# Score matmuls as TensorE loops with a register-held address, in the middle pairs of three layers

## The chip, the cores and the metric

The kernel runs on one core of one Trainium2 chip. The metric is the device time of one execution in microseconds (us); three runs of the kernel before took 1979.33, 1980.79 and 1981.32 us, so its median is 1980.79 us. A core has five engines that run their own instruction streams and meet through semaphores: TensorE (PE, with its weight loads shown apart as PEld), VectorE (DVE), ScalarE (ACT), GpSimd (POOL) and SyncE (SP), which here issues the transfers from the chip's memory (HBM) to 16 DMA engines.

## What is computed

Four layers of attention for one token, A and B in turn: layer 0 is A, 1 is B, 2 is A again and 3 is B again. Each has 32 heads of 192 values and a cache of 8192 keys and values per head.

```python
def _A_ref(x, k_cache, v_cache, wq, wo):
    B, Sq, D = x.shape                      # 1, 1, 640
    q = (x @ wq).reshape(B, Sq, Hq, Dh) ... # Hq 32, Dh 192
    scores = jnp.einsum("bhqd,bhkd->bhqk", q, k) * (Dh ** -0.5)
    p = _softmax(scores, axis=-1)
    o = jnp.einsum("bhqk,bhkd->bhqd", p, v)
    return (o, back to one row) @ wo

x = x + _A_ref(_layernorm(x), A_k_cache, A_v_cache, A_wq, A_wo)
x = x + _B_ref(_layernorm(x), B_k_cache, B_v_cache, B_wq, B_wo)
x = x + _A_ref(_layernorm(x), A_k_cache, A_v_cache, A_wq, A_wo)
x = x + _B_ref(_layernorm(x), B_k_cache, B_v_cache, B_wq, B_wo)
```

Nearly all of the data is the caches, in bf16: with the weights, one execution reads 848 MB.

## The kernel before

**Pairs.** The 32 heads are worked on two at a time: `NPAIR` is 16 pairs per layer. The two heads of a pair lie on partitions 0 to 63 and 64 to 127; each partition holds `J` = 128 keys of 192 values. A pair's keys (6144 KB) fill two of the eight slots of the SBUF tensor `pool` (`NSLOT`, `slot`), one for each half `u` of `JU` = 64 keys per partition, and its values fill two more. So two pairs' worth of caches fit on the chip at once.

**The order.** The list `steps` (L245 to L304) sets what the engines do: for a pair `p` the scores of both halves (`products(p, 0)` and `products(p, 1)`), then `softmax(p)`, `values(p)` and `gather(p)`, then the next pair. Each engine's instructions are collected in a `Queue` in that order, with the semaphore waits that precede each of them (`Queue.settle` writes a wait into the list unless an earlier one covers it; `emit` sends them out). The list `plan` is the same for the transfers, all of which go through SP's queue; a transfer waits until the last reader of its slots has finished (`freed`, `before`). The keys of a pair are released by the last score matmul of a half (`freed[nt]`, L692), the values by the last matmul of `values` (L798).

**`products(p, u)`** (L663) is the part that is changed. VectorE multiplies the half's keys by the query, in place, in `NC` pieces along the 192 values of a head: two pieces of 96 in the middle pairs (`2 <= p < 14`) of layers 0, 1 and 3, four pieces of 48 elsewhere (L671). A piece is one instruction (L675). Then TensorE adds the products up: each matmul with the identity `ident` as its weights takes `R` = 8 of the 192 columns of all 64 keys (512 elements) and adds them into the PSUM bank `S` of that half. That is 12 matmuls per piece and 24 per half, each written out as an instruction of its own; before each piece PE waits for VectorE's piece (L683). The first matmul of a pair carries a weight load (L690); the others use `matmul_held` (L70 to L75), which adds a matmul without loading the weights again, so in the profile nearly all of them have the line L72. Their first one clears the bank (`start`), their last one signals.

**After the scores**, VectorE's reduction (L733, of both halves) sums the last 8 partial sums of every key, further small steps of DVE, PE and ACT make the softmax, PE multiplies the probabilities with the values (L790 and L72, tile `OY`), and VectorE folds the result (L814 and L816). VectorE executes in order, so its multiplication for the next pair (L675) stands behind L816 of this one. `q_spread` (L580) puts the next pair's query into PSUM; on PE it stands right behind the last score matmul.

Of the kernel before, what the change touches and what calls it, by code (L numbers as in the profile page):

```python
# [11 lines left out]
class Queue:  # L12
# [26 lines left out]
            for i, v in [(k, val), *implied[k].items()]:  # L39
                self.waited[i] = max(self.waited.get(i, 0), v)  # L40

    def op(self, fn, *events, sem=None, inc=1, signal=True, bank=(), holds=None):

        self.holds = holds
        for d in bank:
            self.wait(*[ev for q, ev in d.items() if q is not self])
        self.wait(*events)
        self.settle()
        if not signal:
            self.items.append((fn, None, 0))  # L50
            return None
        sem = self.sem if sem is None else sem
        n = self.counts[id(sem)] = self.counts.get(id(sem), 0) + inc
        self.known[id(sem), n] = dict(self.waited)
        self.items.append((fn, sem, inc))
        for d in bank:
            d[self] = (sem, n)
        return sem, n
# [11 lines left out]
def matmul_held(t, out, lhsT, rhs, start, stop, size=128, column=0):  # L70

    return t.add_instruction(mybir.InstMatmult(  # L72
        name=t.bass.get_next_instruction_name(), engine=mybir.EngineType.PE,
        ins=[t.lower_ap(rhs), t.lower_ap(lhsT, for_matmul_weights=True)], outs=[t.lower_ap(out)],
        start_tensor_calc=start, stop_tensor_calc=stop, tile_size=(128, size), tile_position=(0, column), ldweights=False))  # L75


PAIRS_W = 5
NSLOT = 8
# [3 lines left out]
def build(nc, A_x, A_k, A_v, A_wq, A_wo, B_x, B_k, B_v, B_wq, B_wo, out):  # L83
    _, H, SK, DH = A_k.shape
# [8 lines left out]
    R = 512 // JU  # L93
# [5 lines left out]
    TS = JU * DH  # L99
# [12 lines left out]
    with ExitStack() as ctx:  # L112
        def sb(name, shape, dt):
            return ctx.enter_context(nc.sbuf_tensor(name, shape, dt))
# [4 lines left out]
        def sem(name):  # L119
            return ctx.enter_context(nc.semaphore(name))  # L120

        ident = sb("ident", [P, P], BF16)
        pool = sb("pool", [P, NSLOT * TS], BF16)
        slot = [pool[:, i * TS:(i + 1) * TS] for i in range(NSLOT)]
        wq0 = [sb(f"wq0{i}", [P, DC, PD], BF16) for i in range(2)]
        rows = sb("rows", [P, QR], BF16)
# [49 lines left out]
        Su = [(use["S0"],), (use["S1"],)]  # L176
# [6 lines left out]
        PE = Queue(sem("pPE"))  # L183
# [8 lines left out]
        e = PO.op(lambda g: g.memset(ident[:], 0.0))  # L192
# [6 lines left out]
        e = PO.op(lambda g: g.memset(mask, 0.0))  # L199
        for t in range(G):  # L200
            e = PO.op(lambda g, t=t: g.affine_select(
                out=mask, in_=mask, compare_op=ALU.not_equal, fill=1.0,
                base=-32 * t, pattern=[[-1, 2], [-2, VK]], channel_multiplier=1), e)
# [7 lines left out]
        e = DV.op(lambda v: v.tensor_reduce(half[:], mask, AX.X, ALU.add), ev_mask)  # L211
# [7 lines left out]
        def first_load(kind, l, p):  # L219

            n = (kind, pair(l, p))
            if l >= 2 and n in KEPT[l - 2]:
                return (l - 2, ORDER[l - 2]["pairs"].index(n[1]))
            return (l, p)

        def stays(kind, l, p):
            return l < 2 and (kind, pair(l, p)) in KEPT[l]
# [17 lines left out]
        for l in range(NL):  # L245
# [8 lines left out]
            for p in range(NPAIR):  # L254
# [21 lines left out]
                if p < NPAIR - 2:  # L276
                    if first_load("v", l, p) == (l, p):
                        plan += [("v", l, p, u) for u in range(2)]
                        if l == 2 and p == 1:
                            i = plan.index(("k", l, 1, 0))  # L280
# [4 lines left out]
                    if p + 1 in (PAIRS_W, 2 * PAIRS_W):  # L285
                        b = (p + 1) // PAIRS_W - 1
# [18 lines left out]
        at = {n: i for i, n in enumerate(steps)}  # L305
# [11 lines left out]
        place, before, holder = {}, {}, [None] * NSLOT  # L317
# [31 lines left out]
        for g, (c0, k) in enumerate(Q_PARTS):  # L349
            i = plan.index(("wq", 2, g))  # L350
# [6 lines left out]
        for i, n in list(enumerate(plan)):  # L357
            if n[0] == "v" and n[3] == 0:
                m = n[:3] + (1,)
# [87 lines left out]
        def need(n):  # L447

            while n not in landed:
                m = plan[issued[0]]  # L450
                issued[0] += 1
                landed[m] = transfer(m)
            return landed[n]
# [22 lines left out]
        def busy(n):  # L476

            PE.wait(ev_const, last["S"][0])
            for i in range(n):
                PE.op(lambda t, i=i: (  # L480
                    t.matmul(SP_[0][:, :], lhsT=ident[:], rhs=ident[:].unsqueeze(1).broadcast_to([P, 4, P]), start=True, stop=True)
                    if i == 0 else
                    matmul_held(t, SP_[0][:, :], ident[:], ident[:].unsqueeze(1).broadcast_to([P, 4, P]), True, True)),
                    signal=False, bank=Su[0])
# [14 lines left out]
        def layer(l, ev_z, ev_true):  # L499
# [7 lines left out]
            if l == 2:  # L507
                busy(2)
            e = DV.op(lambda v: v.scalar_tensor_tensor(out=nv[:], in0=mv[:, 0:1], scalar=mv[:, 0:1], in1=mv[:, 1:2],
                                                       op0=ALU.mult, op1=ALU.subtract))  # L510
            e = DV.op(lambda v: v.tensor_scalar(vs[:], nv[:], -float(DH), float(DH) * EPS, ALU.mult, ALU.add), e, last["rs"])
# [6 lines left out]
            if l < 2:  # L518
                e = need(("wq", l, 0))
# [4 lines left out]
            else:  # L524
                e = ev_first[l - 2]
                q_first = wq0[l - 2]
            PE.wait(e)
            for c in range(DC):
                e = PE.op(lambda t, c=c: t.matmul(
                    QM[:, 0:PD], lhsT=xb[:, c:c + 1].broadcast_to([P, P]), rhs=q_first[:, c, :],  # L530
                    start=(c == 0), stop=(c == DC - 1)), signal=(c == DC - 1), bank=QMu)
# [131 lines left out]
            def products(p, u):  # L663
                nk = ("k",) + first_load("k", l, p) + (u,)
                nt = ("t", l, p, u) if stays("k", l, p) else nk
                kin = slot[place[nk]].rearrange("p (j d) -> p j d", d=DH)
                k3 = slot[place[nt]].rearrange("p (j d) -> p j d", d=DH)
                qi = (l * NPAIR + p) % 2
                DV.wait(need(nk), need(nt), ev_q[p])
                chunks = []  # L670
                NC = 2 if l != 2 and 2 <= p < NPAIR - 2 else 4  # L671
                QD = DH // NC
                for c in range(NC):
                    d0 = c * QD
                    e = DV.op(lambda v, d0=d0: v.tensor_tensor(  # L675
                        k3[:, :, d0:d0 + QD], kin[:, :, d0:d0 + QD],
                        q_sb[qi][:, d0:d0 + QD].unsqueeze(1).broadcast_to([P, JU, QD]), ALU.mult))
                    chunks.append(e)
                last["q"][qi] = chunks[-1]
                S = SP_[u]  # L680
                PE.wait(last["S"][u], ev_const)
                for c in range(NC):
                    PE.wait(chunks[c])  # L683
                    for r in range(QD // R):
                        d0 = c * QD + r * R
                        fin = c == NC - 1 and r == QD // R - 1
                        held = PE.holds is ident
                        e = PE.op(lambda t, d0=d0, fin=fin, held=held: (
                            matmul_held(t, S[:, :], ident[:], k3[:, :, d0:d0 + R], d0 == 0, fin) if held else
                            t.matmul(S[:, :], lhsT=ident[:], rhs=k3[:, :, d0:d0 + R], start=d0 == 0, stop=fin)),  # L690
                            signal=fin, bank=Su[u], holds=ident)
                freed[nt] = ev_S[p, u] = e  # L692
# [149 lines left out]
            for n in [n for n in steps if n[1] == l]:  # L842
                if n[0] == "m":
                    products(*n[2:])
                elif n[0] == "s":
                    softmax(n[2])
# [19 lines left out]
                elif n[0] == "wo":  # L866
                    k = NW - NB[l] if n[2] == 2 else NW
                    if l == 3 and n[2] == 0:
                        to_row()
                    e = (project_row if l == 3 or n[2] < 2 or NB[l] == 0 else project)(  # L870
                        n, slot[place[n]][:, 0:k * D], oT[:, 0:k], last["oTw"])
# [26 lines left out]
            e = DV.op(lambda v: v.tensor_tensor(x_true[:], x_true[:], YB[:, 0:DC], ALU.add), ev_y, ev_true, bank=YBu)  # L898
# [5 lines left out]
        e = SP.op(lambda s: s.dma_start(out[0, 0].rearrange("(h n) -> h n", h=2), ev_z[0:33:32, :]), ev_true, sem=semOUT, inc=16)  # L904
# [12 lines left out]
def bass_interleave_layers__gqa_block_cached__mha_block_cached__decode_kernel(  # L917
    nc: bass.Bass,
    A_x: bass.AP,
    A_k_cache: bass.AP,  # L920
    A_v_cache: bass.AP,
    A_wq: bass.AP,
    A_wo: bass.AP,
    B_x: bass.AP,
    B_k_cache: bass.AP,
    B_v_cache: bass.AP,
    B_wq: bass.AP,
    B_wo: bass.AP,
    out: bass.AP,
):  # L930
    build(nc, A_x, A_k_cache, A_v_cache, A_wq, A_wo, B_x, B_k_cache, B_v_cache, B_wq, B_wo, out)
# [28 lines left out]
```

## Time and profile before

| what | value |
|---|---|
| median of the runs | 1980.79 us |
| profiled execution | 1979.56 us |
| its span, first to last instruction | 1977.8 us |
| DMA packets of the data queue (q1) | 848.38 MB, 99.7% of the 16 engines' time |
| PE busy | 64% |
| DVE busy | 61% |
| ACT busy | 9% |
| mean granted TensorE clock | 0.789 of full speed |
| one piece of the multiplication (L675, 128x6144) | 3.36 us alone, 13.16 us for a pair's four |
| one issue of keys of 6144 KB, to landing | 34.8 to 35.8 us |

In a row of the profile the line and the engine come first, then the operation with its output and input tiles, the number of instructions, the busy time and the mean of one, and then the engine's idle time ahead of them with what ended it. Busy shares are means over the whole span. Matmuls overlap in their pipeline, so their records (0.38 us for one with 512 columns) are longer than the distance from one to the next. "DVE x <- PE y" in a table of waits means that VectorE stood idle until an instruction of PE was done; the columns are us in total, times, and the longest. Rows marked with a q (PEldq, SPq) are instructions that the engine's sequencer deals with by itself, such as waits on semaphores.

### The profile page before, as it was taken

Reading aid. Unit: us, or ns where it says so; the run is one execution under the profiler, and the core shown is the slowest. Engines: PE = TensorE matmul, PEld = TensorE weight load, DVE = VectorE, ACT = ScalarE, POOL = GpSimd, SP = SyncE. Lnnn points to the kernel's source line nnn. Section 1 sums busy time; section 2 is a strip of 40 time slices with the busy share of each in tenths; the row PEclk is TensorE's granted clock in tenths of the full one; section 3 lists DMA queues with packets and bytes.
Section 4 is the critical chain, followed back from the end, with each engine's and each line's share of the span. In section 5 each row is a group of like instructions: output and inputs, shape, how many; then the busy total and the mean of one; then the engine's idle time right before and its main releaser. Section 6 shows DMA issues by size and latency. Waiting matters only on the chain.

```text
span 1977.8 us, 12008 instructions
## 1 busy us (share of the span) xinstructions
PE 1267.5 (64%) x7742; PEld 127.0 (6%) x2599; DVE 1198.7 (61%) x812; ACT 168.2 (9%) x529; POOL 4.6 (0%) x24
## 2 busy tenths in 40 slices
PE   3567466566476566665786666666666667657668
PEld 0000000000100000000020000000001001000001
DVE  3567467467167656656756565665764765665756
ACT  0000000000000100100010000000000100000000
POOL 0000000000000000000000000000000000000000
PEclk9778787778677787777887777877787878777779
DMA  9999999999999999999999999999999999999998
GB/s 414 431 442 430 430 430 431 435 437 423 433 435 436 431 429 429 432 437 432 428 410 436 427 431 431 433 430 430 432 429 428 435 429 434 439 429 431 432 432 374
DMA packets 27095, 849.12 MB, mean 429 GB/s; under 512 B 3106, under 2 KB 3236, under 8 KB 3876
## 3 DMA queue, kind: packets, MB, share of 16 engines
q1 hardware_dynamic: 26900, 848.38, 99.7%
q8 instruction: 40, 0.66, 0.1%
q14 instruction: 11, 0.09, 0.0%
q10 hardware_dynamic: 144, 0.00, 0.0%
HBM read 848.36 MB, written 0.00 MB: 429 GB/s over the span
## 4 chain that ended last, share of the span: by engine, by line
DMA 58%; PE 25%; DVE 15%; ACT 1%; issue 1%; SPq 0%
DMA pool<-in_B_k_cache_dram 24%; DMA pool<-in_A_v_cache_dram 17%; DMA pool<-in_A_k_cache_dram 15%; PE S L72 14%; DVE pool L675 11%; PE OY L72 5%; PE OY L790 3%; DMA pool<-in_B_v_cache_dram 3%; DVE s_sb L733 1%; ACT p_sb L748 1%; DVE OY L814 1%; PE OY L628 1%; DVE acc L816 1%; PE S L690 1%; DVE m_bf L735 0%
## 5 line engine op out<-in xcount | busy, mean ns | idle before, releaser
L675 DVE TENSOR_TENSOR pool<-pool,q_sb 128x3072 bf16<-128x3072 bf16 (+1 forms) x360 | 837.6, 2392 | 151.0 <-DMA pool<-in_B_k_cache_dram 84.8
L72 PE MATMUL S<-pool,ident 128*128 128x512 bf16 x3004 | 782.9, 422 | 18.1 <-DVE pool L675 16.7
L814 DVE TENSOR_TENSOR OY<-OY,small 128x1536 f32<-128x1536 f32 x60 | 106.0, 1766 | 255.0 <-PE OY L72 254.9
L72 PE MATMUL OY<-pool,p_sb 128*16 128x512 bf16 x1920 | 206.0, 517 | 0.0
L828 PE MATMUL TB<-acc,small 128*33 128x192 f32 x120 | 46.3, 484 | 210.3 <-DVE acc L816 210.3
L733 DVE TENSOR_REDUCE s_sb<-S 128x128 f32<-128x1024 f32 x63 | 77.1, 1224 | 160.0 <-PE S L72 160.0
L690 PE MATMUL S<-pool,ident 128*128 128x512 bf16 x64 | 37.4, 584 | 212.4 <-DVE pool L675 212.3
L790 PE MATMUL OY<-pool,p_sb 128*16 128x512 bf16 (+1 forms) x1216 | 142.6, 490 | 45.3 <-DMA pool<-in_A_v_cache_dram 43.8
L542 ACT ACTIVATE q_sb<-QM 64x192 bf16<-64x192 f32 x120 | 38.9, 324 | 942.4 <-PE QM L580 941.7
L816 DVE TENSOR_REDUCE acc<-OY 128x192 f32<-128x1536 f32 x60 | 105.4, 1757 | 2.0
L837 ACT ACTIVATE rows<-TB,small 1x192 bf16<-1x192 f32 x120 | 49.5, 412 | 557.0 <-PE TB L828 555.5
L748 ACT ACTIVATE p_sb<-s_sb,small 64x128 bf16<-64x128 f32 x128 | 55.7, 435 | 172.1 <-DVE small L742 171.3
L804 DVE RECIPROCAL small<-TB 33x2 f32<-33x2 f32 x64 | 11.1, 173 | 94.3 <-PE TB L763 78.1
L738 PE MATMUL QM<-ident,m_bf 128*64 128x64 bf16 x128 | 14.0, 216 | 82.6 <-DVE m_bf L735 82.6
L763 PE MATMUL TB<-small,ones 128*33 128x2 f32 x120 | 14.4, 190 | 74.1 <-ACT p_sb L748 74.1
L580 PEld LDWEIGHTS QM<-rows,one_b 1*128 1x128 bf16 x60 | 5.5, 91 | 737.0 <-issue 731.0
L790 PEld LDWEIGHTS OY<-pool,p_sb 128*16 128x16 bf16 (+1 forms) x1216 | 34.6, 105 | 195.2 <-issue 138.5
L628 PE MATMUL OY<-pool,oT 128*1 128x320 bf16 x330 | 38.6, 411 | 2.2 <-ACT oT L658 2.2
L742 DVE TENSOR_REDUCE small<-QM 128x1 f32<-128x64 f32 x64 | 14.3, 224 | 27.8 <-PE QM L738 27.8
L828 PEld LDWEIGHTS TB<-acc,small 128*33 128x33 f32 x120 | 10.3, 133 | 297.9 <-DVE acc L816 292.0
L748 ACT ACTIVATION_READ_ACCUMULATOR p_sb<-s_sb,small 64x1 f32 x128 | 23.3, 182 | 0.0
L690 PEld LDWEIGHTS S<-pool,ident 128*128 128x128 bf16 x64 | 6.6, 103 | 249.8 <-DVE pool L675 246.8
(87 smaller groups left out, 245.2 us busy)
## 6 DMA issues: line engine op xcount, KB each, us to landing
pool<-in_B_k_cache_dram SPq DMA_DIRECT2D x28, 6144.0 KB, 35.8
pool<-in_B_v_cache_dram SPq DMA_DIRECT2D x28, 6144.0 KB, 31.0
pool<-in_A_v_cache_dram SPq DMA_DIRECT2D x27, 6144.0 KB, 26.9
pool<-in_A_k_cache_dram SPq DMA_DIRECT2D x34, 3072.0 KB, 20.4
pool<-in_A_k_cache_dram SPq DMA_DIRECT2D x14, 6144.0 KB, 34.8
pool<-in_A_v_cache_dram SPq DMA_DIRECT2D x9, 3072.0 KB, 13.8
pool<-in_B_k_cache_dram SPq DMA_DIRECT2D x8, 3072.0 KB, 22.4
pool<-in_A_wo_dram SPq DMA_DIRECT2D x6, 2400.0 KB, 20.9
```

The lines of the kernel that those rows point to most:

```text
L72: return t.add_instruction(mybir.InstMatmult(name=t.bass.get_next_instruction_name(), engine=mybir.EngineType.PE, ins=[t.lower_ap(rhs), t. ...
L542: lambda a, h=h, r=r, f=f: a.activation(q_sb[i][r, :], QM[r, h * DH:(h + 1) * DH], ACT.Copy, scale=f),
L628: e = PE.op(lambda t, i=i, h=h, f=l < 3 and n[2] == 0 and i == 0, fin=n == last_row and i == k - 1: t.matmul(YR[32 * h:32 * h + 1, :], lhs ...
L675: e = DV.op(lambda v, d0=d0: v.tensor_tensor(k3[:, :, d0:d0 + QD], kin[:, :, d0:d0 + QD], q_sb[qi][:, d0:d0 + QD].unsqueeze(1).broadcast_t ...
L690: t.matmul(S[:, :], lhsT=ident[:], rhs=k3[:, :, d0:d0 + R], start=d0 == 0, stop=fin)),
L733: lambda v: v.tensor_reduce(s[:], S_[:].rearrange("p (j r) -> p j r", r=R), AX.X, ALU.add),
L748: ev_p[p] = AC.op(lambda a, h=h, r=r: a.activation(p_sb[par][r, :, h], s[r, :], ACT.Exp, bias=negm[par][r, 0:1], accum_out=l_col[par][r, h ...
L790: t.matmul(o, lhsT=x, rhs=y, start=f, stop=fin) if c == 0 else
L814: e = DV.op(lambda v: v.tensor_tensor(o3, o3, pick[:, 0:VK].unsqueeze(2).broadcast_to([P, VK, DH]), ALU.mult), bank=Ou)
L816: e = DV.op(lambda v: v.tensor_reduce(acc[:], O.rearrange("p (i d) -> p d i", d=DH), AX.X, ALU.add), e, bank=Ou)
L828: e = PE.op(lambda t: t.matmul(TB[64:97, C_O:C_O + DH], lhsT=half33, rhs=acc[:], start=True, stop=True), bank=TBu)
L837: last["TO"] = last["row_written"] = AC.op(lambda a, h=h: a.activation(orow[:, o0 + h * DH:o0 + (h + 1) * DH], TB[64 + 32 * h:65 + 32 * h, ...
```

## The change

In the pairs with two pieces (12 pairs in each of layers 0, 1 and 3, so 36 pairs, 72 halves and 144 pieces) the matmuls of a piece are no longer all written out. Of a half's 24 matmuls the first and the last stay as they were. The other 11 of each piece are one matmul instruction in a loop on TensorE: its input address is held in the register `k_at0`, which a register addition moves on by 8 columns, and a compare-and-branch goes back until eleven rounds are done. The register is set ahead of the first piece's loop and runs on through the second. The wait for the second piece of the multiplication stands in the loop's body (`inside=True`), so it is executed in each of the eleven rounds; the wait for the first piece belongs to the single matmul ahead of the first loop. `Queue.op` takes the waits out of the list for that purpose and hands them to the function.

```diff
+        at = len(self.items)
         self.settle()
+        if inside:
+            waits, f = self.items[at:], fn
+            del self.items[at:]
+            fn = lambda eng: f(eng, waits)
...
+def matmul_loop(t, waits, out, lhsT, rows, first, count, regs, at, label, begin):
+
+    b, width, m = t.bass, out.shape[-1] // rows.shape[1], len(regs)
+    for i in range(m if begin else 0):
+        t.reg_mov(regs[i], at + 2 * (first + i * width))
+    with b.body(label, valid_engines=[mybir.EngineType.PE]):
+        for w in waits:
+            t.wait_ge(*w)
+        for reg in regs:
+            with b.discard():
+                v = bass.RuntimeValue.of_register_unchecked(reg, min_val=0, max_val=rows.shape[-1] - width)
+                x = t.lower_ap(rows[:, :, bass.ds(v, width)])
+            t.add_instruction(mybir.InstMatmult(
+                name=b.get_next_instruction_name(), engine=mybir.EngineType.PE,
+                ins=[x.__replace__(regref=reg.name, reg_ap_offset=reg.name), t.lower_ap(lhsT, for_matmul_weights=True)],
+                outs=[t.lower_ap(out)], start_tensor_calc=False, stop_tensor_calc=False, tile_size=(128, 128),
+                tile_position=(0, 0), ldweights=False))
+        for reg in regs:
+            t.reg_add(reg, reg, 2 * m * width)
+        t.br_lt(regs[0], at + 2 * (first + count * width), on_true=label, on_false=label + "_end")
+    b.switch_bb(label + "_end")
...
+        pool_at = nc.sbuf_base - 2 * NSLOT * TS
+        k_at = [nc.tensor.alloc_register(f"k_at{i}") for i in range(1)]
...
+                    if NC == 2:
+                        at = pool_at + 2 * TS * place[nt]
+                        n = QD // R
+                        m = len(k_at)
+
+                        def ends(d0):
...
+                        if c == 0:
+                            ends(0)
+                        PE.op(lambda t, waits, c=c: matmul_loop(
+                            t, waits, S[:, :], ident[:], k3, (m + c * (n - m)) * R, n - m, k_at, at, f"k_{l}_{p}_{u}_{c}", c == 0),
+                            signal=False, bank=Su[u], holds=ident, inside=True)
+                        if c == 1:
+                            e = ends(DH - m * R)
+                        continue
```

`ends` writes out the single matmuls (`m` is 1 here, the number of registers) in the form of before, and the last one signals. The arithmetic and its order are unchanged.

## The prediction

> **What bounds the kernel now.** First the page's shares and queues:
>
> ```profile
> PE 1267.5 (64%) x7742; PEld 127.0 (6%) x2599; DVE 1198.7 (61%) x812; ACT 168.2 (9%) x529; POOL 4.6 (0%) x24
> q1 hardware_dynamic: 26900, 848.38, 99.7%
> q8 instruction: 40, 0.66, 0.1%
> DMA 58%; PE 25%; DVE 15%; ACT 1%; issue 1%; SPq 0%
> ```
>
> No engine is full, the data queue is. So the kernel is bound by transfers, and removing work on TensorE can win only what it wins on the DMA engines. But a quarter of the chain of waits is PE: a pair is one serial chain of DVE and PE, and only if this chain is shorter than a pair's transfers does DMA stay the bound. The timeline of two pairs in layer 0 shows the chain:
>
> ```profile
> 95.45 13.16 DVE L675 TENSOR_TENSOR pool<-pool,q_sb 128x6144 bf16<-128x6144 bf16 x4 [2.73 <-DMA pool<-in_A_k_cache_dram]
> ...
> 99.27 12.15 PE L72 MATMUL S<-pool,ident 128*128 128x512 bf16 x47
> ...
> 111.45 1.23 DVE L733 TENSOR_REDUCE s_sb<-S 128x128 f32<-128x1024 f32 x1 [2.84 <-PE S L72]
> ...
> 119.38 1.76 DVE L816 TENSOR_REDUCE acc<-OY 128x192 f32<-128x1536 f32 x1
> ...
> 124.54 13.16 DVE L675 TENSOR_TENSOR pool<-pool,q_sb 128x6144 bf16<-128x6144 bf16 x4 [3.40 <-DMA pool<-in_A_k_cache_dram]
> ```
>
> The reader is to see that pairs start 29.1 us apart, that the next multiplication stands right behind L816, and that VectorE then waits 3.40 us for keys. These few microseconds per pair are all the room a longer chain has. The waits, by stretch (the middle pairs of layers 0, 1 and 3), give the whole of it:
>
> ```profile
> DVE s_sb L733 <- PE S L72: 38.7, 12, 5.1
> DVE pool L675 <- DMA pool<-in_A_k_cache_dram: 33.2, 13, 6.0
> ...
> DVE s_sb L733 <- PE S L72: 43.1, 13, 5.8
> DVE pool L675 <- DMA pool<-in_B_k_cache_dram: 38.1, 14, 8.3
> ...
> DVE s_sb L733 <- PE S L72: 41.0, 14, 3.8
> DVE pool L675 <- DMA pool<-in_B_k_cache_dram: 33.3, 12, 9.5
> ```
>
> VectorE waits (38.7+43.1+41.0)/39 = 3.15 us for the scores after its last piece: they end 13.16+3.15 = 16.3 us after the pair's start. And it waits 33.2+38.1+33.3 = 104.6 us for keys in all.
>
> Last, the pace of the score matmuls, in stretches of one pair (busy time and count of PE, then PEld and DVE; the first figure behind the brackets is the granted clock):
>
> ```profile
> 128.00:131.20 3.20, 3.20 (x8) 0.06 (x1) 0.00 (x0) 0.50 0.92 399
> 131.20:134.50 3.30, 3.30 (x11) 0.00 (x0) 0.00 (x0) 0.66 1.10 477
> 134.50:137.80 3.30, 3.30 (x17) 0.00 (x0) 0.00 (x0) 1.00 1.07 462
> ```
>
> After the idle time TensorE starts at half clock, then runs at full. At full clock 47 matmuls took 10.16 us in the tightest piece of the chain (at 693.46), 0.216 us each, so 0.43 at half. From the clocks 0.50, 0.66 here and 0.50, 0.86 in the pair at 873, some 10 to 13 of 48 matmuls are cold; I take 12. Check: 3.41 (first piece 3.36 and 0.05 to the first matmul) + 12 x 0.43 + 36 x 0.216 + 0.2 (the last one's drain) = 16.5 us, against 16.3 measured. So PE begins behind VectorE (a piece takes 13.16/4 = 3.29 us, 12 matmuls 0.27 us each), and uses its full speed to catch up.
>
> **The change, part by part.**
>
> Instructions removed: per half 24 matmuls become 2 single ones, 2 loop bodies and some set-up, about 12 fewer or a little less; 72 halves save about 900. The queue that feeds PE's instructions brought 0.66 MB for its 10341 records, 64 bytes each, so 0.06 MB less, 0.13 us at 429 GB/s. Bounds: nothing to the whole 0.1% share (2 us); I take 0.
>
> Address register, branch, wait: the loop runs 144 x 11 = 1584 rounds. In a round PE's sequencer deals with the matmul, a register addition, a compare-and-branch and, in the second piece of each half, the wait again. It can run ahead of the array, so a round costs the larger of the array's time and the sequencer's time q. The trace of before has no loop on PE, so q is bounded. Below: the array, 0.216 us. Above: three instructions as slow as the slowest that a sequencer handles here, the DMA issue on SP, 0.33 us: 1.0 us. The nearest rows are these (ns):
>
> ```profile
> L945 PEldq EVENT_SEMAPHORE  x1: 51/51/51, 0.7 to 0.7; - x1
> L945 SPq EVENT_SEMAPHORE  x1: 17/17/17, 0.7 to 0.7; - x1
> L112 SPq COMPARE_BRANCH  x1: 33/33/33, 1977.4 to 1977.4; - x1
> ```
>
> PE's sequencer takes 51 ns where SP's takes 17. A branch of 33 on SP, three times that on PE, is 0.10; addition and matmul at 0.05 each make 0.20, with the wait 0.25. Between consecutive issues SP's sequencer leaves about 0.06 (0.74 + 0.39 = 1.13 to 1.19 at the start of the run); three or four such gaps make q 0.38 to 0.49. I take the middle between 0.20 and 0.49, **0.33 us**, rather than the far bound of 1.0, because the small rows are of the same kind as the loop's instructions and the DMA issue is not.
>
> The Trainium skill (Advanced Engine Details and Errata, Control Flow Timing) puts a compare-and-branch at about 108 ns, near my 0.10; taken with 51 ns each for addition and matmul and no gaps, q would be 0.21 and the loop would cost nothing, which is the first rival's sum.
>
> Loop entry and exit: a register move and the branch that falls through, once each per loop, not shown either; between 0 and 0.33 us, I take 0.2 (four loops per pair, 0.8).
>
> Sum for a pair: 3.41 + 12 x 0.43 + 36 x 0.33 + 0.8 + 0.2 = 21.45 us, so the scores end 21.45 - 16.3 = 5.15 us later. PE no longer catches up with VectorE: in full-clock rounds it needs 0.33 where VectorE's pace is 0.27.
>
> What is late next: L733, the softmax, the values, L814, L816, and behind it on VectorE the next L675; on PE `q_spread` (L580) stands behind the last score matmul but has some 9 us in hand. On SP's queue the values' transfer (released by the scores) and the next keys' transfer (released by the values) are both issued 5.15 us later. A transfer of 6144 KB takes 14.7 us alone and 27 to 36 from issue to landing, so 12 us or more of queued work covers one such delay; it doesn't cover one in every pair.
>
> What hides it: VectorE's waits for keys. To the 104.6 us come 16.3 at the change from layer 0 to 1 and 3.7 in the last pairs, 124.6. Not all can be used (some lie ahead of the first changed pair); I take 115 us, 3.2 per pair. If this cover is gone, every microsecond counts in full. Layer 2 isn't changed.
>
> Total: 36 x 5.15 - 115 = 185 - 115 = +70 us on the profiled 1979.56, so 2050; the median shown is 1.2 above it, so **2051 us**. The sum is steep: 36 x 36 = 1300 us per us of q, or 13 us for every 10 ns. It is nil at q = 0.276, +18 at 0.29, +161 at 0.40.
>
> **The rivals.**
>
> *Hidden* (not slower). The round is within 0.27 us, so PE stays within the waits' cover: at q = 0.25 the scores end 2.3 us later, 83 us in all, less than 115. Time 1979 to 1981. For it: the small rows without gaps sum to 0.20 to 0.25, and DMA at 99.7% hides anything below 3.2 us per pair. Against it: gaps between instructions, and the cold start that uses up the catching-up already. It decides at q = 0.276.
>
> *Half clock.* The array idles within each round, and the granted clock stays at 0.50 through the scores, as it is in their first 3.2 us: a round is 0.43 whatever the sequencer does. 3.41 + 48 x 0.43 + 1.0 = 25.05, 8.75 later, 315 - 115 = +200: 2181 us. For it: at 144.58 the values' matmuls after a paced end ran at 1.07 us for eight where others took 0.60. Against it: in the cold state the array has no gaps at all when q is below 0.43, and the clock rose to 1.00 here although PE waited between pieces.
> The Trainium skill (TensorE: Matmul & The Clock Gate, Part 1) says the clock is raised after a busy window of about 3.4 us and lowered after an idle one; the 3.2 us at 0.50 agree, and by that rule gaps of a third of a round need not lower it, which is why this rival gets less than the forecast.
>
> *Heavy branch.* Going back makes the sequencer start its fetching anew, at about another 0.33 us: q = 0.6, 3.41 + 48 x 0.6 + 1.0 = 33.2, 16.9 later, 608 - 115 = +493, 2474 us. Nothing in the profile of before speaks for it but that no taken branch on PE is shown.
>
> *Faster.* Fewer instruction fetches leave the DMA engines more even; at most the 0.1% of q8 and q14, 2 us: 1979.
>
> **How the numbers follow.** Forecast (q from 0.28 to 0.40, 1985 to 2141 us) 0.49; hidden 0.26; half clock 0.17; heavy branch 0.05; faster 0.03. The likeliest gives 2051. The range goes from 1978, which takes in the hidden case, to 2181, the half clock; left out are the heavy branch, a part beyond the half clock and the small gains. Changes within 0.2% (4 us) can't be told from none in this kernel. Slower: 0.49 + 0.17 + 0.05 = 0.71; within 0.2%: 0.25; faster: 0.04, since a gain of over 4 us would need more than all instruction traffic.
>
> **What the changed profile would show.** The matmuls of the new line follow each other by about 0.33 us at full clock; L733's wait for PE rises from 3.15 to some 8.3 us in the changed pairs; VectorE's waits for keys there fall to nearly nothing; the pairs start 31 us apart instead of 29.1; q1's share falls to about 96%; the chain shows more PE and less DMA; layer 2 (965 to 1515 us) keeps its length. Wrong would be: rounds of 0.22 to 0.27 us with the keys' waits still there (hidden), a clock of 0.5 throughout the scores (half clock), or q8 with more packets than 40 (refetching).

## The result and the profile after

The changed kernel takes 2027.7 us (median of four runs, 2027.04 to 2033.93) against 1980.16 for the kernel before: a ratio of 1.0249, 95% interval 1.0236 to 1.0262 (ratios below are given in the same way, with the interval in brackets). The profiled execution has a span of 2025.2 us, 47.4 more than before. On its page, the queues and the chain of waits:

```profile
q1 hardware_dynamic: 26900, 848.38, 97.8%
q8 instruction: 36, 0.59, 0.1%
PE 50%; DMA 24%; DVE 22%; ACT 3%; issue 1%; SPq 0%
```

The same bytes took a smaller share of a longer span: DMA no longer binds all the time. PE's share of the chain has doubled. The four packets of instructions saved are there (36 instead of 40); the experiments below show whether they are worth anything.

One pair of layer 0, from its timeline (start, duration, engine, line; L95 is the loop's matmul, L77 a single one, L705, L785 and L868 are L675, L733 and L816 of before):

```profile
95.31 13.16 DVE L705 TENSOR_TENSOR pool<-pool,q_sb 128x6144 bf16<-128x6144 bf16 x4 [1.81 <-DMA pool<-in_A_k_cache_dram]
...
99.13 7.73 PE L95 MATMUL S<-pool,ident 128*128 x22
106.71 0.59 PE L77 MATMUL S<-pool,ident 128*128 128x512 bf16 x2
107.14 7.66 PE L95 MATMUL S<-pool,ident 128*128 x22
...
115.06 1.22 DVE L785 TENSOR_REDUCE s_sb<-S 128x128 f32<-128x1024 f32 x1 [6.58 <-PE S L77]
...
127.24 3.35 DVE L705 TENSOR_TENSOR pool<-pool,q_sb 128x6144 bf16<-128x6144 bf16 x1
```

VectorE waits 6.58 us for the scores where it waited 2.84, and the next pair's multiplication, at 127.24, has no wait for keys in brackets: the 3.40 us of before are gone, and the pair lasts 31.9 us instead of 29.1. The waits of all 36 changed pairs, by layer (0, 1 and 3; total, times, longest), say the same:

```profile
DVE s_sb L785 <- PE S L77: 81.3, 12, 7.9
DVE pool L705 <- DMA pool<-in_A_k_cache_dram: 1.8, 1, 1.8
...
DVE s_sb L785 <- PE S L77: 87.3, 12, 11.6
DVE pool L705 <- DMA pool<-in_B_k_cache_dram: 2.2, 2, 1.8
...
DVE s_sb L785 <- PE S L77: 81.4, 12, 8.4
```

VectorE waits (81.3 + 87.3 + 81.4) / 36 = 6.9 us per pair for the scores, and 4.0 us in all for keys, where it was 104.6. The sequencer's own rows, and PE's busy time and count with the granted clock behind them, in four stretches of this pair:

```profile
L101 PEldq ALU_OP  x1584: 36/36/42, 98.8 to 1960.0; - x198
L102 PEldq COMPARE_BRANCH  x1584: 76/208/340, 98.9 to 1960.1; - x198
```

```profile
98.60:104.20 5.60, 5.47 (x14) 0.54 1.00 430
104.20:106.60 2.40, 2.37 (x10) 1.00 1.33 573
106.60:110.60 4.00, 3.98 (x14) 1.00 0.91 393
110.60:114.60 4.00, 3.95 (x12) 1.00 0.97 418
```

The branch is the long one: 208 ns in the median, and 76 in the last round of each of the 144 loops, where it isn't taken. In the trace a round at full clock is 0.363 us: the addition 0.036, a gap of 0.060, the branch 0.207, and 0.06 until the next addition, in which the matmul is sent on. That is longer than the array's 0.216, so PE waits for its own sequencer. The stretches show where that holds (their counts include matmuls that only reach into a stretch). At half clock (the first) a matmul takes the array 0.43 us, so the array is the slower one and the sequencer runs ahead. When the clock rises, at 103.8 us, the matmuls sent ahead start 0.216 us apart until none is left, at 105.1, and from there on it is the sequencer's pace, 0.36 apart within a loop. The sequencer shows no pause while the array is cold: this pair's 44 additions start from 98.82 to 114.43 us, 43 rounds of 0.363 in the mean, and over all 36 pairs this mean has the median 0.362.

By pair, over the 36 changed ones (sums of the trace's start and end times):

| | before | after | difference, us |
|---|---|---|---|
| start of a pair to L733 / L785, mean | 16.49 | 20.10 | 36 x 3.60 = +129.7 |
| from there to the end of L816 / L868, mean | 11.01 | 11.36 | +12.9 |
| from there to the start of the next pair, sum | 86.5 | -1.4 (records overlap) | -87.9 |
| the rest: mostly waits at the change from layer 0 to 1 | | | -7.2 |
| span | 1977.8 | 2025.2 | +47.4 |

In the second row it is the matmuls with the values that grew. In this pair, before (the first line) and after, eight of them took:

```profile
115.00 0.60 PE L72 MATMUL OY<-pool,p_sb 128*16 128x512 bf16 x8
118.82 1.07 PE L77 MATMUL OY<-pool,p_sb 128*16 128x512 bf16 x8
```

The granted clock was 1.00 there before, and 0.50 after.

### The profile page after: what moved, and what is told of

Read it like the earlier page. It is cut to its first block, busy times and chain, and to the rows that moved or that the text cites. A ratio compares the mean times of both kernels' runs of the same rounds, so it can differ in the third digit from the quotient of the medians.

```text
span 2025.2 us, 15248 instructions
## 1 busy us (share of the span) xinstructions
PE 1407.0 (69%) x7742; PEld 129.9 (6%) x2599; DVE 1195.4 (59%) x812; ACT 168.1 (8%) x529; POOL 4.6 (0%) x24
## 3 DMA queue, kind: packets, MB, share of 16 engines
q1 hardware_dynamic: 26900, 848.38, 97.8%
## 4 chain that ended last, share of the span: by engine, by line
PE 50%; DMA 24%; DVE 22%; ACT 3%; issue 1%; SPq 0%
PE S L95 25%; DMA pool<-in_A_v_cache_dram 14%; DVE pool L705 11%; PE OY L77 7%; PE S L77 6%; DMA pool<-in_A_k_cache_dram 5%; DMA pool<-in_B_k_cache_dram 5%; PE OY L842 5%; DVE OY L866 4%; DVE acc L868 4%; DVE s_sb L785 3%; ACT p_sb L800 2%; PE OY L658 2%; PE S L725 1%; DVE m_bf L787 1%
## 5 line engine op out<-in xcount | busy, mean ns | idle before, releaser
L705 DVE TENSOR_TENSOR pool<-pool,q_sb 128x3072 bf16<-128x3072 bf16 (+1 forms) x360 | 836.9, 2391 | 63.9 <-DMA pool<-in_A_k_cache_dram 36.0
L95 PE MATMUL S<-pool,ident 128*128 x1584 | 536.7, 430 | 4.5 <-issue 2.2
L77 PE MATMUL S<-pool,ident 128*128 128x512 bf16 x1420 | 382.2, 421 | 10.5 <-DVE pool L705 9.8
L785 DVE TENSOR_REDUCE s_sb<-S 128x128 f32<-128x1024 f32 x63 | 77.1, 1224 | 291.8 <-PE S L77 291.8
L77 PE MATMUL OY<-pool,p_sb 128*16 128x512 bf16 x1920 | 214.8, 537 | 0.0
L842 PE MATMUL OY<-pool,p_sb 128*16 128x512 bf16 (+1 forms) x1216 | 151.1, 520 | 43.4 <-DMA pool<-in_A_v_cache_dram 43.4
L868 DVE TENSOR_REDUCE acc<-OY 128x192 f32<-128x1536 f32 x60 | 105.4, 1757 | 2.0
L725 PE MATMUL S<-pool,ident 128*128 128x512 bf16 x36 | 21.3, 593 | 78.3 <-DVE pool L705 78.3
L790 PE MATMUL QM<-ident,m_bf 128*64 128x64 bf16 x128 | 14.1, 218 | 82.6 <-DVE m_bf L787 82.6
L742 PE MATMUL S<-pool,ident 128*128 128x512 bf16 x28 | 16.0, 570 | 53.6 <-DVE pool L705 53.6
## 6 DMA issues: line engine op xcount, KB each, us to landing
pool<-in_A_k_cache_dram SPq DMA_DIRECT2D x14, 6144.0 KB, 29.9
```

The source lines that it names most:

```text
L77: return t.add_instruction(mybir.InstMatmult(name=t.bass.get_next_instruction_name(), engine=mybir.EngineType.PE, ins=[t.lower_ap(rhs), t. ...
L95: t.add_instruction(mybir.InstMatmult(name=b.get_next_instruction_name(), engine=mybir.EngineType.PE, ins=[x.__replace__(regref=reg.name, ...
L705: e = DV.op(lambda v, d0=d0: v.tensor_tensor(k3[:, :, d0:d0 + QD], kin[:, :, d0:d0 + QD], q_sb[qi][:, d0:d0 + QD].unsqueeze(1).broadcast_t ...
L725: t.matmul(S[:, :], lhsT=ident[:], rhs=x, start=f, stop=fin)), signal=fin, bank=Su[u], holds=ident)
L785: lambda v: v.tensor_reduce(s[:], S_[:].rearrange("p (j r) -> p j r", r=R), AX.X, ALU.add),
L842: t.matmul(o, lhsT=x, rhs=y, start=f, stop=fin) if c == 0 else
```

## The experiments

The theory: the sequencer's round, above all its branch, sets the pace of the score matmuls, and what the scores' lateness costs is its sum over the pairs less VectorE's waits for keys. The rivals: the register-held address makes the matmul itself slow; and every round costs its share of the 47.4 us wherever it stands. Times stand against runs of the kernel before on the same chip: 1979.42 us for the first four, 1979.71 for the others.

**What in the round costs: the branch removed.** The eleven matmuls and additions are written out, with the same register. The wait of a second piece then stands once ahead of its matmuls instead of in every round.

```diff
-    with b.body(label, valid_engines=[mybir.EngineType.PE]):
-        for w in waits:
-            t.wait_ge(*w)
+    for w in waits:
+        t.wait_ge(*w)
+    for k in range(count // m):
         for reg in regs:
...
-        t.br_lt(regs[0], at + 2 * (first + count * width), on_true=label, on_false=label + "_end")
-    b.switch_bb(label + "_end")
```

> The same register-held matmuls and register additions written out, no branch. If the branch sets the round, the sequencer needs 0.363 - 0.208 - 0.05 = about 0.10 us per matmul with its addition, the array's 0.216 binds, and the time is that of the kernel before, 1978 to 1983 us. If the register-held address or the addition is what costs, it stays near 2028 us.

It took 1981.04 us, ratio 1.0008 (0.9998 to 1.0017): no difference shown, and at most 0.17%. The second half of the same pair (L783 is the L785 of the changed kernel):

```profile
107.47 4.91 PE L95 MATMUL S<-pool,ident 128*128 x22
112.22 0.38 PE L77 MATMUL S<-pool,ident 128*128 128x512 bf16 x1
112.63 1.23 DVE L783 TENSOR_REDUCE s_sb<-S 128x128 f32<-128x1024 f32 x1 [3.74 <-PE S L77]
```

The 22 register-held matmuls took 4.91 us, 0.216 apart, where the loop's took 7.66. The register-held address and the addition are free here; the branch is not.

**Two matmuls per round.** `for i in range(2)` in the line of `k_at`: five rounds of two matmuls per piece.

> Two registers, so two matmuls per round and five rounds per piece. If the branch sets the round (a round of 0.363 us, of which the branch and the gaps around it are all but one matmul's dispatch of 0.06 and one addition's 0.10), a round of two takes 0.363 + 0.06 + 0.10 = 0.52 us, 0.26 per matmul, below VectorE's 0.274: scores end at most 1 us later than in the kernel before, the time is 1980 to 1984 us. If the matmul with a register-held address is itself slow, two of them take 0.7 us, and the time stays near 2028. If each executed round costs a fixed 0.030 us (47.4 us over 1584 rounds), 720 rounds cost 22 us: 2002.

It took 1980.1 us, ratio 1.0003 (0.9993 to 1.0012). Its sequencer and the same pair's timeline:

```profile
L101 PEldq FUSED_REGOPS  x720: 37/37/42, 99.2 to 1909.8; - x180
L102 PEldq COMPARE_BRANCH  x720: 69/201/333, 99.3 to 1909.9; - x180
```

```profile
99.87 6.87 PE L95 MATMUL S<-pool,ident 128*128 x20
106.58 1.03 PE L77 MATMUL S<-pool,ident 128*128 128x512 bf16 x4
107.44 4.48 PE L95 MATMUL S<-pool,ident 128*128 x20
```

The branch takes as long as ever, but the two additions became one instruction, and consecutive branches start 0.37 us apart: the second matmul, with its addition, costs the sequencer 0.01 us, not the 0.06 + 0.10 expected. At 0.19 per matmul the array binds: the last 20 looped matmuls run at 0.216 each, and the scores are at L785 16.8 us after this pair's start (95.62).

**Three matmuls per round.** `range(3)`: three rounds per piece.

> Three registers: three matmuls per round, three rounds per piece. The branch is shared by three, the array binds, and the time is that of the kernel before and of two registers: 1978 to 1982 us. If fewer instructions to fetch were worth something, this or the kernel of two registers would be below the kernel before by more than 1 us; I expect that neither is.

It took 1979.7 us, ratio 0.9998 (0.9989 to 1.0008). Neither loop that keeps up is faster than the kernel before.

**A second addition per round, next to the first.** The addition is split into two in a row.

```diff
-            t.reg_add(reg, reg, 2 * m * width)
+            t.reg_add(reg, reg, m * width)
+            t.reg_add(reg, reg, m * width)
```

> The loop of the changed kernel with its addition done in two halves: one more sequencer instruction per round. If the sequencer's round is the bound and VectorE's waits are already used up, the round grows by about 0.10 us (an addition of 0.036 and its gap of 0.06), 44 rounds per pair by 4.3 us, 36 pairs by 154: 2182 us. If rounds are bound by the array, or by something that runs beside the additions, nothing changes: 2028.

It took 2027.43 us, ratio 1.0245 (1.0228 to 1.0262), as the changed kernel. This is no evidence for the second case of the expectation: the trace has 1584 additions, one per round, so the two had been combined and the question stayed open.

**A second addition, apart from the first.** Half a step is added ahead of the matmul and half behind it, and the register starts half a step lower.

```diff
-        t.reg_mov(regs[i], at + 2 * (first + i * width))
+        t.reg_mov(regs[i], at + 2 * (first + i * width) - width)
...
+            t.reg_add(reg, reg, m * width)
             with b.discard():
...
-            t.reg_add(reg, reg, 2 * m * width)
-        t.br_lt(regs[0], at + 2 * (first + count * width), on_true=label, on_false=label + "_end")
+            t.reg_add(reg, reg, m * width)
+        t.br_lt(regs[0], at + 2 * (first + count * width) - width, on_true=label, on_false=label + "_end")
```

> One addition of half a step ahead of the matmul and one behind it, so that two additions stand in every round and can't be combined (in the trace of the run with the addition split in two, each round still had one). If the sequencer's round is the bound, it grows from 0.363 by 0.036 and a gap of about 0.06 to 0.46 us; 44 rounds per pair are 4.3 us, 36 pairs 154 us, with no cover left: 2182 us. If something else than the sequencer sets the round, the time stays near 2028.

It took 2237.54 us, ratio 1.1305 (1.1286 to 1.1324). The same pair:

```profile
L92 PEldq ALU_OP  x1584: 36/36/42, 99.0 to 2167.5; - x198
```

```profile
109.93 10.17 PE L96 MATMUL S<-pool,ident 128*128 x22
120.00 0.38 PE L77 MATMUL S<-pool,ident 128*128 128x512 bf16 x1
...
120.41 1.23 DVE L786 TENSOR_REDUCE s_sb<-S 128x128 f32<-128x1024 f32 x1 [11.72 <-PE S L77]
```

The direction and the kind are as expected, the size is larger: 36 ns of addition lengthen a round to 0.475 us, and every third or fourth one to 0.515; that is 0.12 more on average instead of 0.097, and VectorE now waits 11.72 us. The scores end 8.9 us later than before in the mean, 319 us in all. Added to the changed kernel's 2027.7, 36 x 44 x 0.12 = 190 us of longer rounds and 18 us of growth between the scores and the end of the pairs make 2236. The sequencer's round is the bound; what makes an addition ahead of the matmul dearer than one behind it was not tried.

**Which rounds cost: the last piece plain.** Loops in three of a pair's four pieces.

```diff
-                    if NC == 2:
+                    if NC == 2 and (u, c) != (1, 1):
```

> The last of a pair's four pieces written out, the other three as loops. If only the moment counts at which the scores end, the last 12 matmuls at 0.216 us end 1.4 us earlier than with a loop, 18.3 us after the pair's start, 1.8 later than before; 36 x 1.8 = 65 us is less than VectorE's waits for keys gave (about 90), so the time is 1980 to 1990 us. If every round costs its share, three quarters of 47.4 remain: 2016 us.

It took 1984.22 us, ratio 1.0022 (1.0013 to 1.0032): a quarter of the rounds removed took away nine tenths of the loss. The same pair's last piece:

```profile
107.42 3.73 PE L95 MATMUL S<-pool,ident 128*128 x11
111.00 2.75 PE L77 MATMUL S<-pool,ident 128*128 128x512 bf16 x12
113.78 1.23 DVE L785 TENSOR_REDUCE s_sb<-S 128x128 f32<-128x1024 f32 x1 [5.02 <-PE S L77]
```

The eleven looped matmuls follow each other by (111.00 - 107.42) / 11 = 0.325 us, twelve of them would be 3.9; the twelve plain ones, at 0.216, are 2.6. The written-out end wins back 1.3 us, and the scores are done 18.2 us after this pair's start (95.60).

**Loops in the first half only** (`if NC == 2 and u == 0:`).

> Loops in the first half of each pair only, half of all rounds. If only the end of the scores counts, PE is late by about 2 us after the first half, catches up with the second half at 0.216 us per matmul and ends about 0.8 us later than before: 36 x 0.8 = 29 us, covered by VectorE's waits for keys: 1979 to 1983 us. If every round costs its share, 2004 us.

It took 1979.85 us, ratio 0.9999 (0.9990 to 1.0009): half of the rounds at no cost. The scores end 0.85 us later in the mean, and the waits for keys take that.

**Loops in every other pair** (`if NC == 2 and p % 2 == 0:`).

> Loops in every other of the middle pairs: 18 pairs whose scores end 3.6 us later, 65 us in all, as much as in the run with the last piece plain (1984 us), but in half as many pairs. If the waits of neighbouring pairs can be used too (transfers are queued ahead by 12 us or more, so a late pair is made up for in the next), the time is again 1980 to 1988 us. If a pair's lateness can only be covered by its own wait of 2.4 us, 18 x 1.2 = 22 us are lost: 2002 us. If every round costs its share, 2004.

It took 1989.46 us, ratio 1.0050 (1.0033 to 1.0066). It has as many rounds as the run before it, but they are not free; the time is far below the 2002 of a cover within each pair alone, and just above the 1980 to 1988 expected. In the profiled execution the scores' lateness sums to 73.5 us and the 36 pairs last 1084.5 us; with the last piece plain it was 72.6 and 1085.3. Waits of 2.4 us in the late pairs alone would have covered 43 us and left 30 as loss; it was 10, so neighbours do share their waits. The 5 us between the two medians stay open.

Put together, with the lateness of the scores (summed over the 36 pairs, against the kernel before) and the loss in the runs:

| kernel | lateness, us | loss, us | looped rounds |
|---|---|---|---|
| first half only | 30.4 | 0.1 | 792 |
| last piece plain | 72.6 | 4.8 | 1188 |
| every other pair | 73.5 | 9.8 | 792 |
| changed kernel | 129.7 | 47.5 | 1584 |
| two additions apart | 319.3 | 257.8 | 1584 |

The loss follows the lateness, not the number of rounds. Where the waits for keys are gone, it is the lateness and the growth of the rest of the pairs less some 95 us: for the changed kernel 129.7 + 12.9 - 47.4 = 95, for two additions apart (where the rest grew by 31 us) 319 + 31 - 256 = 94 by the profiles. The cover isn't a sharp edge: the last piece plain and every other pair still have 11 and 13 us of waits ahead of their next pairs, and lose 5 and 10 us already.

## Why the prediction was right

The forecast (slower, for the chain of a pair) was right, and 2027.7 us lies in its own range of 1985 to 2141; +70 was said, +47.4 came. The mechanism held. That the number came this close is in part luck: the lateness was put 56 us too high (185 for 129.7), the cover 20 too high (115 for 95), and 12.9 us of growth were not in the sum. By its steps:

- **The bound changes from DMA to the pair's chain**: shown. The pairs start 1131.1 / 36 = 31.4 us apart (31 said; before, the mean was 29.9, and the 29.1 of the prediction is one pair's), VectorE's waits for keys are nearly gone (4.0 us), q1 fell to 97.8% (some 96 said), and layer 2 is as long as before within 1.2 us. L785's wait is 6.9 us where 8.3 was said.
- **The round, q**: 0.33 said, 0.363 measured. Taking rows from small sequencer instructions was right in size, but the parts were not: the branch is 0.207 instead of 0.10, the addition 0.036 instead of 0.05, and there are two gaps of 0.06 instead of three or four, with the matmul sent on in one of them. The upper bound of 1.0 us was misread: 0.33 us is the usual DMA issue on SP, not the slowest (others took 0.39 to 0.63, one 1.2). The Trainium skill (Advanced Engine Details and Errata, Control Flow Timing) has about 108 ns for a compare-and-branch; on PE this trace shows 208 taken and 76 not taken, and the sum of 0.21 us by that rule would have meant a loop at no cost, which did not come.
- **The sum for a pair** is the step that was mis-sized: 21.45 us, 5.15 later; the scores end at 19.73 in the median, 3.6 later in the mean. With the measured round the sum would have been 22.6, so it has 3 us too much elsewhere. The cold matmuls don't stand in series with the rounds: while the array is at half clock the sequencer runs ahead, and the matmuls sent ahead then follow at the array's speed (0.8 us too much). The four single matmuls were charged a round each, 1.45 us, though they are in no loop. And the ends were put at 1.0 us. The sequencer's rounds alone give the measured end: 3.5 us to the first addition, 43 rounds of 0.362 to the last one, and 0.6 from there to L785 are 19.7. A round that was too short and these three charges that were too high went against each other.
- **The cover**: 115 us said, 95 used. Of the 16.3 us counted at the change of layers little came back: the 13.4 us wait for the first keys of layer 1 is as long as before, and it was the wait for that layer's query weights that shrank, from 14.1 to 7.6 us.
- **Not foreseen**: +12.9 us between the scores and the end of a pair. The values' matmuls of the pair shown took 1.07 us for eight, at half clock, where the kernel before has 0.60. By the traces' clock records the clock was at half for 34% of these stretches before, for 42% in the changed kernel and for 54% with two additions apart, where they grew by 31 us: the growth goes with the clock. Kernels whose loops keep up show some of it too (36 to 38% and 11.2 to 11.3 us a pair, against 11.01), so it isn't the loop's alone; why the clock is lower there is open.
- **The rivals**: hidden would have needed a round of 0.276. Half clock fell for the scores: the clock is 1.00 from 104.2 us on in the stretches above, though the array has work for 0.216 us of a round of 0.363, and 0.798 in the mean of the whole run. The 3.2 us at 0.50 that the prediction sets beside the busy window are the length of the stretch shown, not of the cold time: by its own two rows, 0.50 and then 0.66, the clock stayed at half for some 5.4 us. Heavy branch fell: q8 has fewer packets, and a taken branch is 0.13 us longer than one that falls through, not 0.33. Faster fell too: no loop that keeps up was faster than the kernel before.

## What to carry to other kernels

A loop on TensorE is paced by the larger of the array's time and the sequencer's round, and one taken branch with an addition and its gaps took 0.36 us here: with two or three 512-column matmuls in a round (0.216 us each) the loop cost nothing. What a slower producer costs is read from the moment at which its last result is done, less the consumer's waits for something else: 792 rounds in the first halves of the pairs were free, since a second half at the array's pace followed; 792 rounds in every other pair, with nothing behind them to catch up, cost 10 us. On a kernel at 99.7% of its DMA time these waits (2.4 us of 29.9 per pair) are the whole margin, so they are the first thing to add up.

## What was not expected of the hardware

- A branch costs 76 ns or 208 on PE, by whether it goes back; the second register-held matmul in a round, with its addition, cost the sequencer 0.01 us, against 0.363 for the round around the first.
- The wait in the loop's body costs nothing: it has no instruction of its own in the trace (the second loop's matmuls carry it), and rounds of 0.36 us are found in loops with it and without it.
- Two additions of different registers stand in the trace as one instruction of 37 ns, and two of the same register as one addition; whether the chip or the building of the program joins them is not shown. Ahead of the matmul, one more addition of 36 ns cost 0.12 us per round.
